# Transposing gathered expert rows by crossbar DMA instead of on TensorE

## The chip, the cores and the metric

The kernel runs on one core of a Trainium2 chip. The time is device microseconds of the core; each figure is a median of several executions. The span of a profile is about 1.8 us shorter than the time of the same execution.

## The reference

Two stages: attention with a band and eight global columns, then a mixture of eight experts. Only the second matters here. The routing gives each expert exactly 3072 / 8 = 384 tokens.

```python
# q, k, v: (4, 8, 768, 64); attention output -> x: (3072, 512)
def _moe_ref(x, w_gate, w1, w2):
    logits = x @ w_gate                       # 8 experts
    ...                                       # greedy assignment by score, cap 384 tokens an expert
    for e in range(E):
        mask = assigned == e
        h = np.maximum(x[mask] @ w1[e], 0.0)  # w1[e]: 512 x 1024
        out[mask] = h @ w2[e]                 # w2[e]: 1024 x 512
```

## The kernel before

The kernel's products sum over the partitions of their operands, so the rows of an expert (tokens on partitions, 512 features along the free axis) must be transposed before the first product. A gather on GpSimd fetches a block of 128 token rows, `xe` (128 x 512 bf16, 128 KB). TensorE transposes it in four 128 x 128 matmuls against an identity, into PSUM (`pxe`), and VectorE copies the result to SBUF (`xT`). An expert has three such blocks. Experts 0 to 3 have their first block done early, during routing, and so have two left in the last stage; experts 4 to 7 have three. That makes 20 blocks in the expert stage and four early ones.

```python
# NKC = 4 (512/128), NFC = 8 (1024/128), TSLAB = 3 blocks of 128 tokens, EX = 4
gp = ...tile_pool(name="gp", bufs=11, ...)    # gathered rows
fp = ...tile_pool(name="fp", bufs=2, ...)     # their transposes

def experts(first):
    ...
    def load_x(e):
        xT_e = fp.tile([128, NKC, TSLAB, 128], BF16, tag="xT_e", name=f"xT_{e}")
        for j, t in enumerate(slabs(e)):
            xe = xes.pop(TSLAB * e + t)
            pxe = ps_t.tile([128, NKC, 128], BF16, tag="pxe")
            for kc in range(NKC):
                nc.tensor.transpose(pxe[:, kc, :], xe[:, 128 * kc : 128 * kc + 128], ident_bf)
            nc.vector.tensor_copy(out=xT_e[:, :, j, :], in_=pxe)
        xT_of[e] = xT_e
    ...
    for e in range(N_EXP):
        ahead = 3 if first else 2
        if e + ahead < N_EXP and not (first and e + ahead < EX):
            gather(e + ahead, slabs(e + ahead))   # GpSimd's queue
        if first:
            late_weights()                        # one 1 MB load, also GpSimd's queue
        ...                                       # 8 x 4 matmuls ph <- w1, xT; ScalarE: hT <- relu(ph)
        if e + 1 < N_EXP:
            load_x(e + 1)
        ...                                       # per block: 8 matmuls po <- hT, w2; eviction; scatter
```

`gather`, `late_weights` and the scatters all issue on GpSimd's queue. SyncE's queue carries plain loads and stores.

The softmax here doesn't subtract the row's maximum and nothing guards it: scores larger than these inputs give would overflow.

## Time and profile before

| | before |
|---|---|
| time, median (range) | 264.21 us (264.09 to 264.97) |
| span of the profiled execution, mean granted clock | 262.4 us, 0.990 |
| first matmul of expert 0's late rows to the end of the last `po` matmul | 180.22 to 253.56: 73.34 us |
| waits of TensorE over 0.3 us in that stage | none |
| from there to the end of the span | 8.84 us |

I call the third row the expert stage.

Queue q0 is GpSimd's, q1 SyncE's.

### The profile page before, as it was taken

To read this page: it belongs to the slowest core of one execution; us is meant where nothing else is said; L and a number is where in the kernel's file an instruction comes from. 1 tells how busy PE (TensorE), PEld (TensorE's weight loads), DVE (VectorE), ACT (ScalarE), POOL (GpSimd) and SP (SyncE) were. 2 spreads that over 40 slices of the span, in tenths; PEclk is the share of its full clock that TensorE was granted. 3 is DMA by queue.
4 is the path that set the end of the run, shared out by engine and by line. 5 is a ranking of instruction groups with operands and counts; after the bars stand their busy time and mean duration, and the time that the engine had idled before them with its cause. 6 is when DMAs were issued, how large, how long until landed. Compare 5 with 4: busy or idle time off the path is not lost.

```text
span 262.4 us, 7770 instructions
## 1 busy us (share of the span) xinstructions
PE 243.1 (93%) x3299; PEld 178.4 (68%) x3299; DVE 163.4 (62%) x346; ACT 142.6 (54%) x241; POOL 87.1 (33%) x145
## 2 busy tenths in 40 slices
PE   8699979999999999999998899998999999999960
PEld 2567867888788887887877676666666665555520
DVE  3987998897978979689854878751233223223120
ACT  5998959689496895953523232234333351432500
POOL 5050000030260772023018100157863875641240
PEclk9999999999999999999999999999999999999996
DMA  7995599759799699939996999923899999991221
GB/s 261 328 290 105 169 223 231 186 119 260 170 243 240 158 279 150 206 77 164 212 209 134 182 209 214 192 69 111 143 217 280 246 185 263 216 291 59 95 84 46
DMA packets 52570, 49.29 MB, mean 188 GB/s; under 512 B 29745, under 2 KB 44081, under 8 KB 52529
## 3 DMA queue, kind: packets, MB, share of 16 engines
q0 software_dynamic: 15680, 26.22, 48.8%
q1 hardware_dynamic: 36848, 22.50, 33.7%
q8 instruction: 28, 0.46, 0.8%
q14 instruction: 14, 0.11, 0.1%
HBM read 56.05 MB, written 9.44 MB: 250 GB/s over the span
## 4 chain that ended last, share of the span: by engine, by line
PE 61%; DVE 17%; issue 9%; ACT 4%; POOL 4%; DMA 2%; POOLq 0%; SPq 0%; DVEq 0%
PE po L435 11%; PE ps L382 10%; PE ph L1360 9%; PE po L1369 7%; PE pr L466 7%; DVE RT L322 4%; PE pk L511 4%; DVE P L415 4%; POOL out_dram L931 4%; PE poE L974 3%; DMA RT<-in_q_dram 2%; PE pr L469 2%; DVE qT L347 2%; PE phE L958 1%; PE pxe L1339 1%
## 5 line engine op out<-in xcount | busy, mean ns | idle before, releaser
L400 ACT ACTIVATE P<-ps 128x860 f32<-128x860 f32 (+1 forms) x46 | 39.3, 893 | 23.3 <-PE ps L382 22.5
L1363 ACT ACTIVATE hT<-ph 128x256 bf16<-128x256 f32 (+1 forms) x64 | 27.9, 436 | 42.1 <-PE ph L1360 40.4
L382 PE MATMUL ps<-qT,kA 32*128 32x215 f32 (+2 forms) x864 | 43.6, 333 | 2.6 <-ACT qT L347 2.6
L382 PEld LDWEIGHTS ps<-qT,kA 32*128 32x128 f32 x864 | 37.2, 185 | 7.3 <-ACT qT L347 3.1
L435 PE MATMUL po<-P,v 128*64 128x215 f32 (+6 forms) x576 | 41.5, 293 | 0.2 <-DVE P L415 0.2
L435 PEld LDWEIGHTS po<-P,v 128*64 128x64 f32 x576 | 33.9, 136 | 8.7 <-issue 3.7
L415 DVE TENSOR_TENSOR P<-P,Wm 128x860 f32<-128x860 f32 (+1 forms) x32 | 32.9, 1043 | 6.7 <-ACT P L400 4.0
L931 POOL DMA_INDIRECT out_dram<-ot,idi x20 | 19.6, 982 | 27.2 <-DVE ot L1376 20.3
L1376 DVE COPY ot<-po 128x512 f32<-128x512 f32 x19 | 13.1, 691 | 24.8 <-PE po L1369 23.9
L322 DVE STREAM_TRANSPOSE RT<-RT 128x768 f32<-128x768 f32 x28 | 26.2, 959 | 3.4 <-DMA RT<-in_k_dram 3.3
L466 PE MATMUL pr<-P,onesx 128*32 128x192 f32 (+11 forms) x768 | 27.6, 259 | 0.0
L1340 DVE COPY xT<-pxe 128x512 bf16<-128x512 bf16 x20 | 7.8, 421 | 31.6 <-PE pxe L1339 30.9
L466 PEld LDWEIGHTS pr<-P,onesx 128*32 128x32 f32 x768 | 24.7, 109 | 2.3 <-issue 0.3
L1369 PEld LDWEIGHTS <-hT 128*128 128x128 bf16 x160 | 15.2, 98 | 16.2
L1369 PE MATMUL po<-w,hT 128*128 128x512 bf16 x112 | 25.6, 379 | 0.0
L1360 PE MATMUL ph<-xT,w 128*128 128x384 bf16 (+1 forms) x160 | 25.1, 315 | 0.0
L332 ACT COPY kA<-RT 128x720 f32<-128x720 f32 (+2 forms) x18 | 24.3, 1353 | 0.1
L1360 PEld LDWEIGHTS <-w 128*128 128x128 bf16 x160 | 15.7, 98 | 9.3
L923 POOL DMA_INDIRECT xe<-x_tok,idi x20 | 19.2, 961 | 7.6 <-issue 3.7
L408 DVE TENSOR_TENSOR P<-P,Wm 128x860 f32<-128x860 f32 x16 | 16.5, 1060 | 7.1 <-ACT P L400 7.1
L440 ACT COPY oT<-po 128x384 f32<-128x384 f32 x32 | 14.8, 491 | 11.1 <-PE po L435 11.1
L511 PE MATMUL pk<-ident,oT 128*128 128x128 f32 x96 | 16.5, 287 | 2.1 <-DVE LT L482 2.0
(232 smaller groups left out, 315.7 us busy)
## 6 DMA issues: line engine op xcount, KB each, us to landing
w<-in_moe_w_dram POOLq DMA_DIRECT2D x10, 1024.0 KB, 12.4
v<-in_v_dram SPq DMA_DIRECT2D x32, 180.0 KB, 3.3
RT<-in_k_dram SPq DMA_DIRECT2D x7, 768.0 KB, 4.5
RT<-in_q_dram SPq DMA_DIRECT2D x7, 768.0 KB, 7.3
w_early<-in_moe_w_dram POOLq DMA_DIRECT2D x8, 512.0 KB, 8.3
x_tok<-x SPq DMA_DIRECT2D x32, 96.0 KB, 3.3
RT<-in_moe_w_dram POOLq DMA_DIRECT2D x2, 1024.0 KB, 18.8
w_early<-in_k_dram SPq DMA_DIRECT2D x1, 768.0 KB
```

The lines of the kernel that those rows point to most:

```text
L322: nc.vector.transpose(out=t, in_=src[:, :, 32 * g : 32 * g + 32])
L332: nc.scalar.copy(out=kA[:, i0:i1, 8:128].rearrange("p i (c j) -> p i c j", j=NJ), in_=t[:, i0 * NC5 : i1 * NC5, :].rearrange("p (i c) j -> ...
L382: nc.tensor.matmul(heads[a][:, o : o + w], lhsT=kA[r, gd, i, :], rhs=qTt[r, gd, KT * i : KT * i + w], start=(gd == 0), stop=(gd == 1), ski ...
L400: nc.scalar.activation(P[:, :, 0 : GW[g]], ps[w_][:, :, 0 : GW[g]], AF.Exp, scale=0.125)
L415: tt(out=P[:, :, 0 : GW[g]], in0=P[:, :, 0 : GW[g]], in1=Wm[:, h0 : h0 + 2, lo : lo + GW[g]], op=ALU.mult)
L435: nc.tensor.matmul(po[n][bk][64 * t : 64 * t + 64, a - QB * bk : z - QB * bk], lhsT=v7[:, t, i, :], rhs=P[:, t, o + a - q0 : o + z - q0], ...
L466: nc.tensor.matmul(o_, lhsT=l_, rhs=r_, start=first[gq], stop=True, skip_group_check=True)
L511: nc.tensor.transpose(pk[:, bb, :], oTs[n][:, 3 * hf + bb].rearrange("c g r -> c (g r)"), ident)
L931: s = nc.gpsimd.indirect_dma_start(out=out[:, :], out_offset=bass.IndirectOffsetOnAxis(ap=ids, axis=0), in_=ot, in_offset=None)
L1360: nc.tensor.matmul(ph[:, 0 : 128 * ns], lhsT=w1_of(e)[:, kc, 128 * fc : 128 * fc + 128], rhs=xT_e[:, kc, 0:ns, :].rearrange("p t n -> p (t ...
L1363: nc.scalar.activation(hT[:, fc, 0 : 128 * ns], ph[:, 0 : 128 * ns], AF.Relu)
L1369: nc.tensor.matmul(po, lhsT=hT[:, fc, 128 * j : 128 * j + 128], rhs=w2_of(e)[:, fc, :], start=(fc == 0), stop=(fc == NFC - 1))
```

## The change

The intent: take the transposes out of TensorE's gapless stream, and their copies from VectorE, by letting the DMA transpose while it moves the rows from one place in SBUF to another (`dma_start_transpose`, called crossbar DMA below). Expert 0 stays on TensorE. Seven experts' blocks, 18 in the last stage and 3 early ones, go through SyncE. The pool of rows shrinks from 11 to 8 buffers to make room for a third buffer of transposed rows, because a transpose now starts two experts ahead.

```diff
+            for e in range(1, EX):
+                nc.sync.dma_start_transpose(out=xT_early[e], in_=xe_early[e])
 ...
-    gp = ...tile_pool(name="gp", bufs=11, ...)
-    fp = ...tile_pool(name="fp", bufs=2, ...)
+    gp = ...tile_pool(name="gp", bufs=8, ...)
+    fp = ...tile_pool(name="fp", bufs=3, ...)
 ...
+    def turn(e):
+        x_tile(e)
+        for j, t in enumerate(slabs(e, True)):
+            nc.sync.dma_start_transpose(out=xT_of[e][:, :, j, :], in_=xes.pop(TSLAB * e + t))
 ...
         def rows(e):                    # early transposes of TensorE
             def go():
+                if e:
+                    return
 ...
                 gather(e, slabs(e, True), False)   # end of routing
+            x_tile(0)
+            for e in range(1, 3):
+                turn(e)
 ...
             for e in range(N_EXP):
 ...
+                if first and e + 2 < N_EXP and e > 0:
+                    turn(e + 2)
 ...
-                if e + 1 < N_EXP:
+                if e + 1 < N_EXP and not first:
                     load_x(e + 1)
```

More of the change, by code (lines that the diff above doesn't have):

```diff
@@ L891 @@
     late_tiles(w2pool, range(3, N_EXP - 2))
-    gp = xctx.enter_context(tc.tile_pool(name="gp", bufs=11, reuse_waits="tile"))
-    fp = xctx.enter_context(tc.tile_pool(name="fp", bufs=2, reuse_waits="tile"))
+    gp = xctx.enter_context(tc.tile_pool(name="gp", bufs=8, reuse_waits="tile"))
+    fp = xctx.enter_context(tc.tile_pool(name="fp", bufs=3, reuse_waits="tile"))
     hp = xctx.enter_context(tc.tile_pool(name="hp", bufs=2, reuse_waits="tile"))
@@ L916, with slabs @@
     xes = {}
+    xT_of = {}
     scatters = []
+    def slabs(e, first):
+        return range(1 if first and e < EX else 0, TSLAB)
     def gather(e, slabs, pin=True):
@@ L928, in gather, with x_tile @@
             xes[s] = xe
+    def x_tile(e):
+        xT_of[e] = fp.tile([128, NKC, TSLAB, 128], BF16, tag="xT_e", name=f"xT_{e}")
+    def turn(e):
+        x_tile(e)
+        for j, t in enumerate(slabs(e, True)):
+            nc.sync.dma_start_transpose(out=xT_of[e][:, :, j, :], in_=xes.pop(TSLAB * e + t))
     def scatter(ot, ids):
@@ L1293, in routing @@
             for e in range(EX):
-                gather(e, range(1, TSLAB), False)
+                gather(e, slabs(e, True), False)
+            x_tile(0)
+            for e in range(1, 3):
+                turn(e)
             late_weights(False)
@@ L1327, in experts @@
             ps_o = fctx.enter_context(tc.tile_pool(name="ps_o", bufs=3, space=bass.MemoryType.PSUM))
-            xT_of = {}
-            def slabs(e):
-                return range(1 if first and e < EX else 0, TSLAB)
             def load_x(e):
-                xT_e = fp.tile([128, NKC, TSLAB, 128], BF16, tag="xT_e", name=f"xT_{e}")
-                for j, t in enumerate(slabs(e)):
+                xT_e = xT_of[e] if first else fp.tile([128, NKC, TSLAB, 128], BF16, tag="xT_e", name=f"xT_{e}")
+                for j, t in enumerate(slabs(e, first)):
                     xe = xes.pop(TSLAB * e + t)
@@ L1343, in experts @@
             if not first:
-                gather(0, slabs(0))
+                gather(0, slabs(0, False))
             load_x(0)
             if not first:
-                gather(1, slabs(1))
+                gather(1, slabs(1, False))
             for e in range(N_EXP):
                 xT_e = xT_of.pop(e)
-                ns = len(slabs(e))
+                ns = len(slabs(e, first))
                 ahead = 3 if first else 2
                 if e + ahead < N_EXP and not (first and e + ahead < EX):
-                    gather(e + ahead, slabs(e + ahead))
+                    gather(e + ahead, slabs(e + ahead, first))
+                if first and e + 2 < N_EXP and e > 0:
+                    turn(e + 2)
                 if first:
@@ L1363, in experts @@
                     nc.scalar.activation(hT[:, fc, 0 : 128 * ns], ph[:, 0 : 128 * ns], AF.Relu)
-                if e + 1 < N_EXP:
+                if e + 1 < N_EXP and not first:
                     load_x(e + 1)
-                for j, t in enumerate(slabs(e)):
+                for j, t in enumerate(slabs(e, first)):
                     po = ps_o.tile([128, DM], FP32, tag="po")
```

## The prediction

> **What bounds the kernel now.** I read the page's busy shares first, then the chain of work that ended last, then TensorE's timeline in the expert stage, then the table of stretches with the DMA share, and last the DMA issues with their times to landing.
>
> The busy shares, and the group of the copies that the change removes:
>
> ```profile
> PE 243.1 (93%) x3299; PEld 178.4 (68%) x3299; DVE 163.4 (62%) x346; ACT 142.6 (54%) x241; POOL 87.1 (33%) x145
> ...
> L1340 DVE COPY xT<-pxe 128x512 bf16<-128x512 bf16 x20 | 7.8, 421 | 31.6 <-PE pxe L1339 30.9
> ```
>
> TensorE is busy 93% of the span. VectorE spends 7.8 us on the 20 transposed-block copies, and sat idle 30.9 us waiting for TensorE's transposes: there VectorE follows, TensorE leads. TensorE's timeline of one expert boundary and one three-block expert:
>
> ```profile
> 202.17 3.66 PE L1360 MATMUL ph<-xT,w 128*128 128x256 bf16 x32
> 205.66 0.61 PE L1339 MATMUL pxe<-ident_bf,xe 128*128 128x128 bf16 x8
> 206.11 0.59 PE L1369 MATMUL po<-w,hT 128*128 128x512 bf16 x2
> 206.57 0.38 PE L1339 MATMUL pxe<-ident_bf,xe 128*128 128x128 bf16 x4
> 206.79 3.18 PE L1369 MATMUL po<-w,hT 128*128 128x512 bf16 x14
> 209.81 5.36 PE L1360 MATMUL ph<-xT,w 128*128 128x384 bf16 x32
> ```
>
> No row has a wait in brackets, and the rows adjoin; that holds from 180.2 to the last matmul near 253.5. So from 180 us on TensorE alone sets the end, and whatever leaves its stream shortens the kernel, if the next input is there. After it comes a fixed tail: last eviction at 254.1, last scatter issued at 254.7, span end 262.4.
>
> What else runs in that stage, in the table of stretches (start:end, length, busy time of each engine, clock, DMA share, GB/s):
>
> ```profile
> 175.00:185.00 10.00, 8.96 (x69) 6.00 (x67) 1.80 (x6) 4.66 (x11) 7.62 (x11) 1.00 0.36 106
> 185.00:205.00 20.00, 20.00 (x150) 13.90 (x149) 5.66 (x10) 8.04 (x22) 12.27 (x14) 1.00 1.08 220
> 205.00:232.00 27.00, 27.00 (x173) 15.17 (x172) 8.38 (x16) 8.98 (x19) 18.43 (x20) 1.00 1.06 222
> 232.00:262.00 30.00, 21.56 (x125) 11.48 (x123) 5.75 (x10) 8.21 (x17) 7.14 (x8) 0.92 0.31 113
> ```
>
> The last two columns matter: from 185 to 232 us the DMA engines are full (1.08, 1.06) with late expert weights, gathers and scatters. The change adds work to just these engines.
>
> **What the Trainium skill says.** (1) "VectorE: DVE Perf Modes", The three transpose paths, gives 390 ns for a 128x128 bf16 transpose on TensorE and 1309 ns by crossbar DMA. The trace shows 219 ns from start to end, but pipelined they cost less: eight start 205.66 and the next matmul starts 206.11, so 0.45 / 8 = 56 ns each. I use 56 ns. (2) "Advanced Engine Details and Errata", X-Bar Transpose (TRN2), calls these DMAs as fast as regular ones; the kernel before has none, so its trace can't say. (3) "DMA: Bandwidth & Descriptors", DMA Transpose (X-bar), has a crossbar tile of 16 partitions by 128 columns of 2-byte data, its source rows 256 bytes. A 128x512 block is then 32 tiles, 512 row pieces, 32 pieces on each of 16 engines. (4) The same page, Queues, rings and completion order: an engine goes round-robin between its queues packet by packet. The trace agrees in kind: the plain SyncE loads and stores land in 3.3 us while gathers queued behind weights on GpSimd's queue need up to 9.6.
>
> **Part by part.**
>
> Removed from TensorE's expert stage: of 80 transposes at line 1339, expert 0 keeps 8. Of the other 72, four (expert 1's first block, at 179.89) lay in a wait for VectorE anyway. The 68 others stood in the gapless stream: 68 x 56 ns = **3.8 us off the path**. Counted by experts 1 to 7: 4 + 8 + 8 + 12 + 12 + 12 + 12.
>
> Removed from VectorE: 18 x 0.42 us = 7.6 us, all off the path. Evictions of po are no longer queued behind them, worth nothing at the end, where no transposes run.
>
> Removed in routing: 12 of 16 early transposes and three ScalarE copies of 0.59 us. At 142.4 to 145.6 VectorE's chain leads: the first routing matmul (144.21) waits for VectorE's logits, the next for later VectorE results. TensorE's early work fills holes there. The placeholders keep their share of the filling budget, so nothing moves up: **0 us**.
>
> Added: 3 + 18 = 21 crossbar DMAs of 128 KB on SyncE's queue. SyncE has little else to do after 126 us but eight x_tok stores. Early ones: gathers end issue at 137.9 to 141.7 and land about 2.7 us after their start, so transposes start near 141 to 144; expert 1's rows are needed near 152, expert 2's at 165. Hidden. Experts 1 and 2, late rows: gathers issue 176.6 to 180.4, land 2.7 us later, in the quiet stretch (share 0.36); transposes should be in by 186 and 188 against needs at 187 and 194. Hidden, expert 1 with little slack.
>
> Expert 4 is the weak place. Its gathers issue from 191.1, behind 1 MB weight loads in the same queue:
>
> ```profile
> 193.68 0.95 POOL L923 DMA_INDIRECT xe<-x_tok,idi  x1 [0.30 <-DMA w<-in_moe_w_dram]
> ...
> xe<-x_tok,idi POOLq DMA_INDIRECT x1, 9.6
> ```
>
> The last lands at 193.68 + 9.6 = 203.3. Expert 4's first matmul was at 209.81; with 20 transposes fewer before it and its own 12 gone it would come at 209.81 - 32 x 0.056 = 208.0. So three crossbar DMAs have about 4.7 us. TensorE needed only 0.67 us for the same. Expert 5's gathers land near 212 for a need near 218.4, expert 6's 219.8 for 228.8, expert 7's 227.1 for 239.2: more room each time.
>
> What one crossbar DMA costs decides. Estimates: if its pieces move as whole packets of some KB, 128 KB at the 220 GB/s of these stretches is 0.6 us, three plus one landing of 3.3 us is about 5 us, so expert 4 waits 0 to 1 us. If every 256-byte piece is its own packet, queue figures of the page give the packet times: SyncE's queue 33.7% of 16 x 262.4 us over 36848 packets = 38 ns; GpSimd's 48.8% over 15680 = 131 ns. Alternating, 32 x (38 + 131) = 5.4 us for one block, some 16 us for three: a wait near 11 us at expert 4, partly repeated later.
>
> Sum, cheap case: -3.8 + 0.5 to 1 of waits = -3 us. Buffers: the row pool falls from 11 to 8, but rows are freed when their DMA has landed and gather 4 reuses rows of experts 0 and 1, done before 190; I charge nothing. Weights: the last w2 load issues at 223.63, takes 10.8 us, lands 234.4, used at 248: 14 us of slack, so delays there stay hidden in the cheap case.
>
> **Rivals.**
>
> A, clean gain: every transpose is hidden, 264.2 - 3.8 = 260.4. For it: SyncE idle, own queue, quiet DMA at 175 to 185. Against: 4.7 us for expert 4 under a full DMA.
>
> B, the wait moves: TensorE stands before expert 4 (perhaps 5) for as long as it gained, 262 to 265. For it: the 9.6 us landing and DMA share over 1. GpSimd's later gathers also wait for earlier DMAs' completion (3.88 us before the scatter at 201.81), so added traffic pushes them too.
>
> C, the DMA becomes the bound: each block takes 4 us or more, three per expert no longer fit in the 10.4 us of matmuls, weights slip, 270 to 280. For it: small pieces and the skill's 1309 ns per 128x128, which times four would be 5.2 us. Against: the same skill calls the crossbar nearly as fast as copies.
>
> **Range and chances.** I give A with small waits half, B a quarter, C a quarter. Median: 264.2 - 3.8 + about 1.9 of waits = 262.3 us. The range for 8 in 10 runs from 260.3, nothing lost, to 271, a mild C. Faster by over 2% needs under 258.9, a gain of 5.3 us, more than the 3.8 the path holds: 0.03. Slower by over 2%, above 269.5: 0.19. Within: 0.78.
>
> **What would show it.** Right: transposes at line 1339 only for expert 0; TensorE's rows adjoin but for a wait before expert 4's first ph named after the xT DMA, under 2 us; the matmul stage from 180 to its end about 3 us shorter; routing unchanged to 0.3 us; crossbar DMAs landing in under 4 us. Wrong: landings of 5 us and more, TensorE waits before experts 5 to 7 as well, weights landing later than 248, or a routing stage stretched because an early transpose is late or holds up an x_tok store on SyncE. A gain over 5 us would mean that something off my list left the path.

## More of the kernel before

The prediction shows the lines that carry the reading. Two rows of the page it does not show are needed later, the granted clock of TensorE in 40 slices (tenths of full speed), and the DMA queues with packets, megabytes and the share of 16 engines' time that the packets took:

```profile
PEclk9999999999999999999999999999999999999996
...
q0 software_dynamic: 15680, 26.22, 48.8%
q1 hardware_dynamic: 36848, 22.50, 33.7%
```

The clock is full until the tail, where TensorE has no more matmuls.

## The result, and the profile after

| | before, same chip | after |
|---|---|---|
| time, median (range), 4 runs each | 264.27 us (264.09 to 264.97) | 282.7 us (281.49 to 284.28) |
| ratio after / before, 95% interval | | 1.0696 (1.0635 to 1.0756) |
| span of the profiled execution, clock | 262.4 us, 0.990 | 279.8 us, 0.956 |
| expert stage | 180.22 to 253.56: 73.34 us | 181.13 to 271.0: 89.87 us |
| waits of TensorE in it | none | 10.00 + 5.72 us |

Ratios, here and below, are the mean time of one kernel's fast runs over that of the other's of the same rounds, so not quite the ratio of the medians that stand beside them. Executions over 1.5% slower than the fastest of the same kernel are left out of the means.

The kernel became 7% slower. The page of the kernel after, with the clock, the queues and the group of the first product (busy us, mean ns of one; idle time before it and what ended it):

```profile
PE 243.9 (87%) x3204; PEld 176.4 (63%) x3215; DVE 156.4 (56%) x328; ACT 141.1 (50%) x238; POOL 87.3 (31%) x145
...
PEclk9799999999999999999999999999998597799997
...
q0 software_dynamic: 15680, 26.22, 46.8%
q1 hardware_dynamic: 48272, 25.26, 41.7%
...
L1377 PE MATMUL ph<-xT,w 128*128 128x384 bf16 (+1 forms) x160 | 29.5, 349 | 15.7 <-DMA xT<-xe 15.7
```

The last line is the answer to the fences of before: TensorE, which adjoined row to row, now stands idle 15.7 us until a transpose DMA lands. VectorE lost its copies (163.4 us busy before, 156.4 now), as intended, and nothing came of it. The clock row shows a dip to 5 where the waits are. Queue q1 has 48272 - 36848 = 11424 packets more, which is 21 x 544: the packet records show each block as 512 packets of 256 bytes and 32 of 4 bytes.

TensorE's timeline from the last two-block expert on (start, length, group, and in brackets the idle time before it and its releaser) shows where the time is lost:

```profile
201.97 3.66 PE L1377 MATMUL ph<-xT,w 128*128 128x256 bf16 x32
205.46 3.62 PE L1386 MATMUL po<-w,hT 128*128 128x512 bf16 x15
219.08 7.99 PE L1377 MATMUL ph<-xT,w 128*128 128x384 bf16 x32 [10.00 <-DMA xT<-xe]
226.90 5.34 PE L1386 MATMUL po<-w,hT 128*128 128x512 bf16 x23
237.97 7.09 PE L1377 MATMUL ph<-xT,w 128*128 128x384 bf16 x32 [5.72 <-DMA xT<-xe]
244.90 5.34 PE L1386 MATMUL po<-w,hT 128*128 128x512 bf16 x23
250.08 5.36 PE L1377 MATMUL ph<-xT,w 128*128 128x384 bf16 x32
```

Two waits, before experts 4 and 5, and after each the same 32 matmuls take longer: 7.99 and 7.09 us against 5.36. The clock records show 0.5 granted for 10.2 us from 214.2 and for 6.8 us from 234.7. TensorE therefore pays for such a wait twice, first by standing and then by resuming at half clock. The Trainium skill describes this ("TensorE: Matmul & The Clock Gate", Part 1: The HAM clock gate): a window of about 3.4 us without activity takes the gate to half clock, and about 3.4 us of activity releases it. The trace agrees in kind, not in each time: half clock came 5.1 us after TensorE stopped for the first wait, but only 2.4 us after it stopped for the second, and full clock 5.4 and 3.6 us after it resumed. Over all the waits before experts 4 to 7 that are shown in this document, those of 3.66 us and more were followed by slow matmuls (6.75 us and more), and those of 3.24 us and less by matmuls of 5.36 us.

The spans differ by 279.8 - 262.4 = 17.4 us. They add up so:

| part | us |
|---|---|
| expert stage starts later (181.13 against 180.22) | +0.9 |
| waits before experts 4 and 5 | +15.7 |
| half clock after them: (7.99 - 5.36) + (7.09 - 5.36) | +4.4 |
| transposes gone: 89.87 - 15.72 - 4.36 = 69.79, against 73.34 | -3.55 |
| tail (8.77 against 8.84) | -0.1 |
| sum | +17.4 |

The first term is the first score matmuls, which took 3.07 us at half clock against 1.92 us before. It was there in some kernels below and absent in others with the same edits, so I don't count it to the change.

The stretches where the waits lie (the columns as in the prediction; last the clock, the DMA share, which is the sum of the packets' times over the time of 16 engines and so can pass 1, and GB/s):

```profile
205.00:232.00 27.00, 16.89 (x76) 8.08 (x76) 2.77 (x4) 4.87 (x11) 16.38 (x17) 0.81 1.22 207
232.00:262.00 30.00, 24.17 (x122) 12.48 (x123) 4.84 (x7) 8.39 (x18) 7.30 (x9) 0.89 0.89 163
```

In 205 to 232 the DMA engines are busier than before (1.22 against 1.06) and move less (207 GB/s against 222), which fits more of their time going into small packets. TensorE is busy 16.89 of 27 us, where it had been busy for all 27.

SyncE's own view of the transposes (ns of issue, then microseconds from issue to landing, each minimum, median and maximum):

```profile
L942 SPq DMA_TRANSPOSE xT<-xe x18: 1188/1298/4641, 180.3 to 243.0; - x18
...
DMA to landing us min/median/max: 11.7/12.5/13.4
```

This landing is no clean measure: the trace gives one for only two of the 18 blocks (those issued at 185.79 and 226.38), and blocks queue behind each other. The packet records are better. For each block, counted by the start of its 512 data packets (an engine that lags puts its last pieces into the next block's count):

| blocks of expert | first issued | first packet | last data packet | us per block |
|---|---|---|---|---|
| 1 and 2 (DMA quiet) | 180.27 | 181.45 | 186.87 | 1.28, 0.88, 0.87, 0.93 |
| 3 | 185.79 | 188.32 | 200.29 | 7.54, 4.42 |
| 4 | 204.76 | 208.56 | 217.79 | 3.28, 2.14, 3.80 |
| 5 | 212.49 | 217.87 | 234.30 | 4.72, 6.42, 5.28 |
| 6 | 226.38 | 234.31 | 244.37 | 3.64, 3.75, 2.65 |
| 7 | 236.43 | 244.37 | 250.93 | 2.46, 3.46, 0.58 |

Two things are to be seen. A block takes about 0.9 us in the quiet stretch and 2.1 to 7.5 us beside the weight loads. And the queue is never idle from 208.56 to 250.34: eleven blocks in 41.8 us, 3.8 us each. Three take 11.4 us, and TensorE uses up an expert's three in 10.4 us (250.08 to 260.46). The transposes are thus a stage of their own that runs a little slower than the matmuls it feeds, besides starting late.

### The profile page after: what moved, and what is told of

It is laid out like the page before. It is cut to its first block, busy times and chain, and to the rows that moved or that the text cites. A ratio compares the mean times of both kernels' runs of the same rounds, so it can differ in the third digit from the quotient of the medians.

```text
span 279.8 us, 7615 instructions
## 1 busy us (share of the span) xinstructions
PE 243.9 (87%) x3204; PEld 176.4 (63%) x3215; DVE 156.4 (56%) x328; ACT 141.1 (50%) x238; POOL 87.3 (31%) x145
## 3 DMA queue, kind: packets, MB, share of 16 engines
q1 hardware_dynamic: 48272, 25.26, 41.7%
## 4 chain that ended last, share of the span: by engine, by line
PE 39%; DMA 16%; issue 14%; DVE 13%; POOL 8%; ACT 7%; POOLq 0%; DVEq 0%
PE po L435 10%; PE ps L382 10%; DMA out_dram<-ot,idi 9%; PE pr L466 6%; DMA w<-in_moe_w_dram 5%; POOL out_dram L945 4%; PE pk L511 3%; POOL xe L929 3%; DVE RT L322 3%; DVE P L415 3%; ACT P L400 2%; DMA RT<-in_k_dram 2%; PE pr L469 2%; ACT kA L332 1%; ACT qT L347 1%
## 5 line engine op out<-in xcount | busy, mean ns | idle before, releaser
L1393 DVE COPY ot<-po 128x512 f32<-128x512 f32 x19 | 13.1, 692 | 75.8 <-PE po L1386 75.8
L382 PE MATMUL ps<-qT,kA 32*128 32x215 f32 (+2 forms) x864 | 44.3, 340 | 1.9 <-ACT qT L347 1.9
L1377 PE MATMUL ph<-xT,w 128*128 128x384 bf16 (+1 forms) x160 | 29.5, 349 | 15.7 <-DMA xT<-xe 15.7
L382 PEld LDWEIGHTS ps<-qT,kA 32*128 32x128 f32 x864 | 37.9, 188 | 6.3 <-issue 2.8
L1377 PEld LDWEIGHTS <-w 128*128 128x128 bf16 x160 | 16.8, 106 | 28.5 <-issue 21.5
L466 PE MATMUL pr<-P,onesx 128*32 128x168 f32 (+11 forms) x768 | 27.6, 259 | 0.0
L1386 PEld LDWEIGHTS <-hT 128*128 128x128 bf16 x160 | 15.7, 98 | 17.6
L1386 PE MATMUL po<-w,hT 128*128 128x512 bf16 x107 | 24.7, 379 | 0.3
L347 ACT COPY qT<-RT 128x768 f32<-128x768 f32 (+1 forms) x11 | 16.6, 1505 | 0.2 <-DVE RT L322 0.2
```

What stands on the lines that cost most here:

```text
L382: nc.tensor.matmul(heads[a][:, o : o + w], lhsT=kA[r, gd, i, :], rhs=qTt[r, gd, KT * i : KT * i + w], start=(gd == 0), stop=(gd == 1), ski ...
L466: nc.tensor.matmul(o_, lhsT=l_, rhs=r_, start=first[gq], stop=True, skip_group_check=True)
L1377: nc.tensor.matmul(ph[:, 0 : 128 * ns], lhsT=w1_of(e)[:, kc, 128 * fc : 128 * fc + 128], rhs=xT_e[:, kc, 0:ns, :].rearrange("p t n -> p (t ...
L1386: nc.tensor.matmul(po, lhsT=hT[:, fc, 128 * j : 128 * j + 128], rhs=w2_of(e)[:, fc, :], start=(fc == 0), stop=(fc == NFC - 1))
```

## The experiments

Sixteen runs were made, in four sets of four, each set with the kernel before beside it. Two sets fell on a chip where the kernel before itself took 275 us (one of its executions took 596 us); those are read only within their set.

**Theory:** each 256-byte piece (a run of bytes that the profile records as one packet) takes its turn with the packets of weights, gathers and scatters, so a block costs 4 us under load and about 1 us without it. The runs below test the cost, the load and the pieces. That packets take turns one by one is not tested: the records don't say which engine a packet ran on. **Rivals:** the smaller pool of rows holds up the gathers; the transposes start too late and only the lead is short; the crossbar itself is slow; everything after expert 4 is only knock-on of the first wait.

### Which blocks cost: quiet, busy, and without the load

*Only the quiet blocks* (experts 1 to 3 by crossbar, 4 to 7 back on TensorE, buffers as after):

```diff
-                if first and e + 2 < N_EXP and e > 0:
+                if first and e == 1:
                     turn(e + 2)
...
-                if e + 1 < N_EXP and not first:
+                if e + 1 < N_EXP and not (first and e + 1 < EX):
                     load_x(e + 1)
```

> The changed kernel with experts 4 to 7 back on TensorE; only the early rows and experts 1 to 3 go by crossbar DMA, in the stretch where the DMA engines are quiet. Theory (the DMA engines' full load makes blocks of experts 4 and 5 late): no TensorE wait in the expert stage, and 20 transposes x 56 ns = 1.1 us off the kernel before, so about 263.1 us (262.3 to 264.2). Rival 'the buffer split 8/3 instead of 11/2 is what hurts': about 280. Rival 'crossbar DMAs are slow or disturbing wherever they run': over 266.

The name fits only in part: expert 3's two blocks already meet the weight loads (7.5 and 4.4 us in the table above), but have lead enough.

Measured: 264.11 us against 264.13, ratio 1.0005 (0.9963 to 1.0048). TensorE's timeline of that kernel, at the boundaries that had the waits:

```profile
202.01 3.66 PE L1377 MATMUL ph<-xT,w 128*128 128x256 bf16 x32
...
209.69 5.36 PE L1377 MATMUL ph<-xT,w 128*128 128x384 bf16 x32
...
220.76 5.36 PE L1377 MATMUL ph<-xT,w 128*128 128x384 bf16 x32
```

No wait and no slow matmuls. The stage takes 72.27 us, 1.07 us less than before; five blocks, 20 transposes, have left it, and 20 x 56 ns is 1.1 us. So the gain is real and of the predicted size. This execution gave it back at its start, by the 0.9 us of half clock named above. The kernel has the pools of 8 and 3 buffers and loses nothing by them. Rows are freed later where all blocks go by crossbar; there the trace of the change has one gather that waited for a transpose, for 0.8 us. So that rival falls.

*Only the busy blocks* (experts 4 to 7 by crossbar, 1 to 3 on TensorE but for their early blocks):

```diff
-            for e in range(1, 3):
-                turn(e)
...
-                if first and e + 2 < N_EXP and e > 0:
+                if first and EX <= e + 2 < N_EXP:
                     turn(e + 2)
...
-                if e + 1 < N_EXP and not first:
+                if e + 1 < N_EXP and not (first and e + 1 >= EX):
                     load_x(e + 1)
```

> The complement: experts 1 to 3 back on TensorE, experts 4 to 7 (and the early rows) by crossbar DMA. Theory: the whole loss stays, 279 to 285 us, with a wait of 7 to 10 us before expert 4 and 3 to 7 us before expert 5. Rival 'it takes the sum of both groups': half the loss, about 272.

Measured: 280.03 us against 264.13, ratio 1.0578 (1.0541 to 1.0614), with waits of 6.5 us before expert 4 and 6.1 us before expert 5:

```profile
216.76 7.35 PE L1375 MATMUL ph<-xT,w 128*128 128x384 bf16 x32 [6.50 <-DMA xT<-xe]
...
235.39 8.26 PE L1375 MATMUL ph<-xT,w 128*128 128x384 bf16 x32 [6.10 <-issue]
```

Nearly the whole loss is in these twelve blocks. The 2.7 us less than the full change go with the shorter wait at expert 4, 6.5 us instead of 10.0.

*Without the load* (the last six weight loads left out, experts 5 to 7 computed with expert 4's weights, wrong results), for the kernel after and for the kernel before:

```diff
     def late_weights(pin=True):
-        if lates:
+        if lates and len(loaded) < 4:
             dst, s_ = lates.pop(0)
+            loaded.append(dst)
...
-        return w1_early[:, e, :, :] if e < W_EARLY else w_late[e][0]
+        return w1_early[:, e, :, :] if e < W_EARLY else w_late[min(e, 4)][0]
```

> The changed kernel without the last six weight loads; experts 5 to 7 use expert 4's weights, so the result is wrong on purpose. Theory (load on the DMA engines): the blocks take about 1.3 us each as in the quiet stretch, TensorE waits under 1 us in all, 260.5 us (259.5 to 262). Rival 'a crossbar DMA itself, or SyncE's issuing of it (1.2 us each), is too slow': over 270.

> Control: the kernel before without the same six weight loads (wrong result on purpose). Theory: these loads are hidden behind TensorE's gapless stream, so nothing changes, 264.2 us (263.5 to 264.6). If they cost something by themselves, it is faster by that much.

Measured: 265.62 us for the changed kernel and 268.24 us for the unchanged one, both against 264.13; ratios 1.0031 (0.9994 to 1.0069) and 1.0159 (1.013 to 1.0187). Both missed their expectations (260.5 and 264.2 us), because both have a tail of 12.7 to 12.9 us instead of 8.8, which I have not explained (the last scatter of the unchanged one goes out at 254.72 us, as before; the extra time comes after it). That is why they are compared with each other: without the load the change gains 2.6 us instead of losing 18. TensorE's timeline of the changed one:

```profile
203.34 3.66 PE L1380 MATMUL ph<-xT,w 128*128 128x256 bf16 x32
...
210.29 5.36 PE L1380 MATMUL ph<-xT,w 128*128 128x384 bf16 x32
...
220.67 5.36 PE L1380 MATMUL ph<-xT,w 128*128 128x384 bf16 x32
```

No wait is left. Its blocks took 0.75 to 2.1 us each (one over 1.4), with the first packet 1.2 to 1.8 us after issue, and SyncE needed 1.2 to 1.3 us to issue each of them, so neither the crossbar nor its issue is slow by itself. The same 18 blocks cost about a quarter when the weights are gone, though gathers and scatters still run. The run removes two things at once, though: gathers no longer queue behind weights, so expert 4's first block goes out at 195.81 instead of 204.76. That the wait is gone is thus due to the rate and the earlier start together; the cost of a block is not touched by this. Its stage is 70.93 us against 73.35, 2.4 us less. One pass of expert 0 ran at half clock (5.12 us against 3.65); without it the gain would be 3.9 us, near the 3.8 that were predicted.

### Is it the pieces or the crossbar?

Copies of the same blocks, without transposition, show what the pieces alone cost. Both give wrong results. One writes 256-byte pieces, the other 1 KB pieces (a whole row):

```diff
-            nc.sync.dma_start_transpose(out=xT_of[e][:, :, j, :], in_=xes.pop(TSLAB * e + t))
+            nc.sync.dma_start(xT_of[e][:, :, j, :], xes.pop(TSLAB * e + t).rearrange("p (c n) -> p c n", n=128))
```

```diff
-        xT_of[e] = fp.tile([128, NKC, TSLAB, 128], BF16, tag="xT_e", name=f"xT_{e}")
+        xT_of[e] = fp.tile([128, TSLAB, NKC, 128], BF16, tag="xT_e", name=f"xT_{e}")
...
-            nc.sync.dma_start_transpose(out=xT_of[e][:, :, j, :], in_=xes.pop(TSLAB * e + t))
+            nc.sync.dma_start(xT_of[e][:, j, :, :], xes.pop(TSLAB * e + t).rearrange("p (c n) -> p c n", n=128))
...
-                                         rhs=xT_e[:, kc, 0:ns, :].rearrange("p t n -> p (t n)"),
+                                         rhs=xT_e[:, 0:ns, kc, :],
```

The last edit lets the first product read the changed layout; its 32 matmuls still take 5.36 us.

> The changed kernel with each of the 18 late crossbar DMAs replaced by a plain SyncE copy of the same block in the same 256-byte pieces (wrong result on purpose). Theory (512 small pieces per block, alternating with GpSimd's packets on full engines): as slow as the change, 278 to 284 us, waits before experts 4 and 5. Rival 'the crossbar itself is the slow part': waits gone, about 261.

> The same with pieces of 1024 bytes, so 128 per block in place of 512 (wrong result on purpose). Theory (number of pieces): a block takes about a quarter of the time under load, near 1 us; what is left is the start of a DMA under load (3.8 us from issue to first packet at expert 4), so a wait under 3 us, 261 to 265 us. Rival 'the latency of a SyncE DMA under load, not the number of pieces': little changed, over 274.

Measured, against a kernel before of 275.31 us: 280.67 us (ratio 1.0182, 1.0154 to 1.0209), and 272.36 us (0.984, 0.9805 to 0.9875). The chip was slower than the first one (the traces of these kernels show stalls in experts 0 and 2 that I have not traced further), and the kernel after was not in the set. So I ran both again with it, unchanged, as the third:

> The changed kernel itself, as the reference of this set, since the last set ran on a chip where the kernel before took 275 us. On a chip where the kernel before takes 264 us: 281 to 284 us. On one like the last: not known, 278 to 292 us.

> Repeat of the plain copy in 256-byte pieces beside the changed kernel. Theory (number of pieces under load): within 3 us of the changed kernel of this set, with waits before experts 4 and 5. Rival 'the crossbar is the slow part': 15 us and more faster.

> Repeat of the plain copy in 1024-byte pieces. Theory: no waits before experts 4 to 7 or under 2 us in all, 260.5 to 263 us where the kernel before takes 264. Rival 'latency of a SyncE DMA under load': within 5 us of the changed kernel.

| same chip, before 274.75 us | crossbar | copy, 256 B | copy, 1 KB |
|---|---|---|---|
| time, median | 287.1 us | 279.14 us | 273.61 us |
| ratio to before, 95% | 1.0438 (1.0382 to 1.0495) | 1.016 (1.0099 to 1.0222) | 0.9953 (0.9903 to 1.0004) |
| wait at expert 4 / at 5 | 4.67 / 5.48 us | 4.13 us / none | none / none |
| blocks of experts 4 to 7 | 3.87 us each, queue never idle | 2.83 us each, queue never idle | 1.2 to 2.6 us, queue idle between experts |
| issue to first packet at expert 4 | 4.1 us | 4.5 us | 4.0 us |

(The means in the row of blocks are 211.34 to 257.72 and 211.71 to 245.72, over twelve blocks each.) TensorE's timelines of the crossbar kernel, of the one with 256-byte copies and of the one with 1 KB copies, on this chip:

```profile
224.62 7.82 PE L1377 MATMUL ph<-xT,w 128*128 128x384 bf16 x32 [4.67 <-DMA xT<-xe]
...
243.10 7.12 PE L1377 MATMUL ph<-xT,w 128*128 128x384 bf16 x32 [5.48 <-DMA xe<-x_tok,idi]
```

```profile
224.18 6.75 PE L1377 MATMUL ph<-xT,w 128*128 128x384 bf16 x32 [4.13 <-DMA xT<-xe]
...
235.95 5.36 PE L1377 MATMUL ph<-xT,w 128*128 128x384 bf16 x32
```

```profile
221.01 5.36 PE L1377 MATMUL ph<-xT,w 128*128 128x384 bf16 x32
226.21 5.34 PE L1386 MATMUL po<-w,hT 128*128 128x512 bf16 x23
231.39 5.36 PE L1377 MATMUL ph<-xT,w 128*128 128x384 bf16 x32
```

(The trace names a gather as what ended the crossbar kernel's second wait. Such names are inferred; the product cannot start before its transposed rows.) The same bytes, copied in 1 KB pieces, leave no wait at experts 4 to 7, on the same queue, beside the same weight loads, with the same late start. So lateness alone is not the fault. But the number of pieces is not the whole of it, nor the larger part: 13.5 us lie between crossbar and 1 KB copy, and only 5.5 of them between the two copies, which differ in their pieces. The other 8 us lie between the crossbar and a copy of equal pieces. I had expected these two within 3 us of each other, and that was wrong: the crossbar adds about 1 us a block under load to what its pieces cost. In the quiet stretch of this set the crossbar took 0.85 to 1.5 us and the copy 0.8 to 1.2.

The packet records show where a part of that 1 us lies. Among the blocks of experts 4 to 7 a 256-byte packet took 41 ns on average by crossbar and 22 ns as a copy, against 18 to 19 ns each in the quiet stretch (32 to 46 ns over four executions by crossbar: the change itself, this one, the busy blocks alone, and the one with four experts' lead on the first chip; 22 ns in both executions of the copies). With 512 packets on 16 engines that is some 0.6 us a block, an estimate that takes the engines as evenly loaded. A crossbar block also has 32 records of 4 bytes where a copy has 16. Why its packets take longer under load, these runs do not show.

### Is it only the lead?

If a block only comes late, gathering four experts ahead instead of three should cure it. I gave the rows that lead, once with one weight load moved later and once with it moved to the early loads:

```diff
-            late_weights(False)              # at the end of routing
...
-                ahead = 3 if first else 2
+                ahead = 4 if first else 2
...
                 if first:
                     late_weights()
+                if first and e == 0:
+                    late_weights()
```

```diff
-    for _ in range(4):
+    for _ in range(5):
         late_weights(False)
...
-            late_weights(False)              # at the end of routing
...
-                ahead = 3 if first else 2
+                ahead = 4 if first else 2
```

> The changed kernel with the gathers of experts 4 to 7 one expert earlier and expert 5's w1 load behind expert 4's gathers, everything else as changed. Theory (crossbar DMAs compete for full DMA engines): expert 4's wait shrinks from 10 to 0 to 4 us, since its blocks may start near 191 in place of 204.8, but the load is the same, so a wait of some us stays or appears at expert 5 or 6: 265 to 274 us. Rival 'the only fault is that expert 4's gathers land late': all waits gone, 260 to 262 us.

> As the last, and expert 5's w1 load goes out with the first four weight loads near 145 us, into the idle DMA stretch that follows 168 us, so 1 MB less competes in the expert stage. Theory: waits under 2 us in all, 260.5 to 263.5 us, a version that may beat both. Rival 'packets of the crossbar DMAs slow everything wherever the weights lie': over 267.

> Repeat of gathers one expert earlier and expert 5's w1 load early. Theory: no waits before experts 4 to 7, the removed 3.8 us of transposes seen, but expert 0's gathers may now queue behind the early weight load (on the last chip 1.4 us and 0.9 us): 261 to 265 us where the kernel before takes 264.

On the slower chip the first settled nothing: it took 278 to 293 us with three of four runs slow, so no ratio is given. The second took 280.78 and, in the second set, 280.66 us (medians that include slow runs; ratios of the fast ones 1.0159, 1.0092 to 1.0226, and 1.0115, 1.0062 to 1.0169), with the profiled execution slow both times. That is a loss both times where I had expected about none or a gain. In the second set its two fast runs, 278.05 and 277.85 us, stand beside the unchanged crossbar kernel at 287.1 us: lead, with one weight load moved away, took back about three quarters of the loss there. A repeat of the first on a chip where before takes 264.32 us is clear:

> Repeat: gathers of experts 4 to 7 one expert earlier. Theory: expert 4's wait falls from 10 us to under 4, a wait of some us stays or turns up at expert 5 or 6; 265 to 276 us where the kernel before takes 264. Rival 'late gathers only': 260 to 262 us.

Measured: 274.6 us, ratio 1.0396 (1.0331 to 1.0461). Its first products of experts 4 to 7:

```profile
209.80 5.36 PE L1378 MATMUL ph<-xT,w 128*128 128x384 bf16 x32 [1.80 <-DMA xT<-xe]
...
225.06 7.04 PE L1378 MATMUL ph<-xT,w 128*128 128x384 bf16 x32 [4.71 <-DMA xT<-xe]
...
240.39 5.36 PE L1378 MATMUL ph<-xT,w 128*128 128x384 bf16 x32 [3.12 <-DMA xT<-xe]
...
251.79 5.36 PE L1378 MATMUL ph<-xT,w 128*128 128x384 bf16 x32 [0.86 <-DMA xT<-xe]
```

Expert 4's blocks are issued at 191.18 instead of 204.76 and its wait falls from 10.0 to 1.8 us, but experts 5, 6 and 7 now wait. From 211.80 to 251.10 nine blocks took 4.4 us each: three need 13.1 us where the matmuls need 10.4. Lead helps, by some 8 us, and does not cure: the queue's rate under load is the rest.

### Expert by expert

Last, the busy blocks in growing sets, counted from the end, where the load stops. In each, experts 1 to 3 and the named ones go by crossbar, the others on TensorE:

```diff
-                if first and e + 2 < N_EXP and e > 0:
+                if first and e > 0 and e + 2 in S:       # S = (1, 2, 3, 7), (1, 2, 3, 6, 7), (1, 2, 3, 5, 6, 7)
                     turn(e + 2)
...
-                if e + 1 < N_EXP and not first:
+                if e + 1 < N_EXP and not (first and e + 1 in S):
                     load_x(e + 1)
```

> Crossbar for experts 1, 2, 3 and 7, TensorE for 4, 5, 6. Theory: expert 7's gathers land near 227, then 3.8 us to the first packet and three blocks of 3.6 us, shorter once the weights end at 236, so ready near 241 for a need near 241: wait 0 to 2 us; stage (first ph to last po) 71.6 to 73.6 against 73.34 us of the kernel before. Rival 'a lead problem of expert 4 alone': no wait, 71.6.

> Crossbar for 1, 2, 3, 6, 7. Theory: expert 6's gathers land near 219.8, ready near 219.8 + 3.8 + 3 x 4 = 235.6 for a need near 230: wait 4 to 8 us before expert 6, stage 76 to 81 us. Rival 'lead problem of expert 4 alone': no wait, stage 71 us.

> The changed kernel with expert 4 alone back on TensorE. Theory: expert 5's gathers land near 212, ready near 212 + 3.8 + 3 x 4.5 = 229 for a need near 218: wait 8 to 12 us before expert 5; stage 80 to 87 us. Rival 'lead problem of expert 4, expert 5 a knock-on': wait under 2 us, stage 71 to 73 us.

| also by crossbar | time (before 264.32 us) | ratio, 95% | waits of TensorE |
|---|---|---|---|
| 7 | 263.94 us | 0.9955 (0.9913 to 0.9998) | 1.45 us (expert 7) |
| 6, 7 | 266.69 us | 1.0058 (1.0014 to 1.0101) | 0.67 (6), 2.94 (7) |
| 5, 6, 7 | 271.35 us | 1.0275 (1.0227 to 1.0323) | 3.24 (5), 3.66 (6) |

The first products of experts 5 and 6 in the last of them:

```profile
222.47 5.36 PE L1377 MATMUL ph<-xT,w 128*128 128x384 bf16 x32 [3.24 <-DMA xT<-xe]
...
236.67 7.04 PE L1377 MATMUL ph<-xT,w 128*128 128x384 bf16 x32 [3.66 <-DMA xT<-xe]
```

The time rises with each expert whose blocks are moved while the weights still load. Without expert 4 in the queue, expert 5 still waits: the rival that all is knock-on of the first wait falls. But 3.24 us is less than the 5.72 of the full change and less than the 8 to 12 that I had expected, which fits a part of expert 5's wait in the full change coming from expert 4's blocks ahead of it. Expert 6's wait in the second version was also overestimated (4 to 8 us expected, 0.67 measured). The version with experts 1, 2, 3 and 7 has the lowest median of all that give right results. Its 0.45% is at the edge of what these runs can tell from nothing, and its profiled execution, the slowest of its four, has a stage of 73.86 us against 73.34 before, so I don't claim it as a faster kernel.

## Why the prediction was wrong

It said 262.3 us with 271 as the upper end; the time was 282.7. Taking its steps in turn:

- **68 transposes at 56 ns, 3.8 us off the path: right.** After the waits and slow matmuls are set aside the stage is 3.55 us shorter. With only five blocks moved, 1.07 us were gained where 1.1 were due.
- **VectorE's copies worth nothing, routing unchanged, buffers free: right.** VectorE is 7.0 us less busy to no effect, and the kernel with only the quiet blocks, which has the new buffers, loses nothing.
- **Experts 1 and 2 hidden: right.** Their four blocks were in by 186.87, needed at 188 and later.
- **Expert 4 as the weak place, with 4.7 us of room: right.** Its first block was issued at 204.76 and TensorE came for it at 209.08, so the room was 4.3 us (3.7 from the landing of its last gather, which came at 205.34, 2 us later than before).
- **"if its pieces move as whole packets of some KB", 0.6 us a block: this is the step that failed.** It was one of two cases and got three quarters of the weight, by way of rivals A and B. The records show 512 packets of 256 bytes, and the run on the chip 3.28, 2.14 and 3.80 us for expert 4's blocks. The other case, 5.4 us a block from alternating 38 and 131 ns packets, had the small pieces right and was 40% high: 3.8 us each over eleven blocks, 2.83 for copies in equal pieces. It put the wait of expert 4 "near 11 us", where 10.0 was measured, but that is partly luck: it had 16 us for expert 4's three blocks where they took 9.2, and left out the 5.1 us before and after them (next point). Its alternation of packets is not shown. The support that the prediction found for turn-taking, SyncE's loads and stores landing in 3.3 us, is a median and no test: the stores whose landing the trace gives took 2.0 to 11.4 us, all before the expert stage. Rival C was what came; its "270 to 280" was still short, as the next two terms are not in it. The sentence that decided against it, that the crossbar is nearly as fast as copies, holds for the quiet stretch at most. Its chances don't fit each other either: C, all of it above 269.5 us, got a quarter, and a time above 269.5 us got 0.19.
- **The landing of 3.3 us added once: under-sized.** Under load the first packet alone comes 3.8 us after the issue (1.2 us in the quiet stretch). Expert 4's 14.3 us are 3.8 to the first packet, 9.2 for the three blocks, and 1.3 to TensorE's start (the last of the third block's 16 completions landed at 218.94, 0.14 us before it).
- **The clock: missing.** Waits this long let the granted clock fall to a half, and 4.4 us went there. The sum had no such term.
- **"more room each time" for experts 5 to 7: wrong for 5.** Its gathers were far enough ahead, but the room was counted against the gathers' landing and not against a queue still filled with expert 4's blocks until 217.79. Fifteen of the sixteen engines had finished expert 5's blocks by 235.5; the last one did at 237.83, and TensorE started at 237.97.
- **Weights "landing later than 248" as a sign of being wrong: it came, and cost nothing.** The last load took 18.4 us instead of 10.8 and landed at 248.2, but the last second product began at 265.66.

What stays open: why the first packet of expert 4 comes 3.8 to 4.5 us after issue under load whatever the pieces; why the crossbar's packets take longer there, and a block about 1 us more, than a copy of equal pieces; the stalls of the slower chip; and the longer tail of the kernels without weights.

## What to carry to other kernels

When work moves from an engine to DMA, count the pieces as well as the bytes, and measure the transfer beside the traffic that it will meet: ask how many packets one transfer makes, on what share the engines already run, and whether the queue's rate, not only its lead, meets what the consumer uses up. Here the trade costs nothing where the DMA is quiet (0.9 us a block), and where the weights load it takes 3.8 us of queue time for 0.22 us of TensorE's. A wait that replaces a short on-path cost can also take the TensorE clock down, so price it as the wait plus the slow matmuls after it.

## What the Trainium skill lacked or had wrong

- "Advanced Engine Details and Errata", X-Bar Transpose (TRN2), calls transposing DMAs as fast as regular ones. From SBUF to SBUF beside other traffic that is not so: 3.87 us a block of 128 KB against 2.83 us for a copy in equal pieces and 1.2 to 2.6 us for a copy in 1 KB pieces, and 287.1 us against 279.14 and 273.61 for the kernel.
- "VectorE: DVE Perf Modes", The three transpose paths, gives one time for each path. Pipelined, a TensorE transpose cost 56 ns of the stream instead of 390, confirmed by 1.07 us for 20; a 128 x 512 crossbar block, which is four 128 x 128 transposes, took 0.87 to 1.28 us with the DMA quiet and up to 7.5 us under load. The table would mislead in both directions.
- "DMA: Bandwidth & Descriptors", DMA Transpose (X-bar), does not say that a block's 256-byte rows each show as a packet (544 records a block here, 32 of them of 4 bytes). The count matters under load: copies in a quarter of the pieces took 1.2 to 2.6 us a block instead of 2.83 and left no wait.
- No page that I read gives the delay from issue to first packet while other traffic loads the DMA: 3.8 to 4.5 us at expert 4, much the same for crossbar and copies, against 1.2 to 1.8 us without the weight loads.
